# A two-headed kernel: the stage that prepares the tables is rewritten, and its rounds get other PSUM places and other side work

## The chip, the core and the metric

The kernel runs on one core of a Trainium2 chip. The metric is device time in microseconds (us), of one launch. PE is the matrix engine (TensorE), DVE the vector engine, ACT the scalar engine, POOL GpSimd, and SP the engine that mostly issues DMAs. SBUF is the on-chip memory, and PSUM is the small memory that matmuls write to: eight banks of 2 KB per partition, handed out here as "places" that must be emptied before they are written again.

## The reference, cut to what matters

Two independent heads, whose outputs are set side by side.

```
# A: 64 segments of 32 rows, one after the other; mem (8 rows) is carried over
h = concat([mem, x[segment]]); q, k, v = h@Wq, h@Wk, h@Wv
p = softmax(mask(q @ k.T * scale)); o = (p @ v) @ Wo
mem = o[:8]; out_a[segment] = o[8:]
# B: a long convolution of u with a kernel K that is made from D x N complex parameters
K[d, l] = Re sum_n C*exp(dt*A*l)*dt*B        # l = 0..2047, d = 0..1023, n = 0..127
y = irfft(rfft(K, 4096) * rfft(u, 4096))[:2048] + u * Dskip
```

Shapes: x and u are 2048 x 1024, the projection weights 1024 x 4096 each, A, B and C 1024 x 128 each, all in bf16.

## The kernel before, in words

The program runs head B first (`part_b`) and head A after it (`part_a`). While B runs, work for A that doesn't depend on the carried memory is done beside it (class `Ahead`): x is transposed, and of each segment the last 8 rows ("left rows", 24 to 31) are multiplied by Wk, Wv and Wq there; the 24 other rows are stored transposed in DRAM (`VXd`) and loaded by part A. Everything is emitted under a manual schedule: each engine runs its instructions in the order in which the code writes them, and so does each queue of DMAs.

The time of `part_b` falls into four stages.

**Parameter stage** (lines 703 to 918). The six parameter arrays are loaded (L710) as 128 partitions x 8 x 128 in pieces of 128 elements. From them DVE and ACT work out, in float32 on 128 x 1024 elements, five quantities: `x1` (decay), `x2` and `x6` (turn of one step, and of 16 steps), `x4` (logarithm of the modulus of C*B*dt) and `x3` (its angle). `put3` (L718) splits each into three bf16 parts, high, middle and low (L720, L723, L725, L729), and writes them to the DRAM tensors `PB`. Small arrays of table rows, `RE` and `RT`, are built by DVE (`rows`, L804, and L821 to L837). `matrices` (L761) makes the Fourier matrices `MF` (16 column groups, cosine and sine, 128 x 512 each): DVE multiplies (L776), ACT rounds (L778), DVE subtracts (L771) and takes absolute values (L767), ACT takes sines (L768, L772). `Ahead.transposes` (L95) loads x in 16 blocks of 128 rows on POOL's queue (L99), PE transposes each block in eight matmuls (L109), ACT copies the 24 other rows of each segment to `xst` (L112) and the left rows to `xTl` (L113), and SP's queue writes `xst` to `VXd` (L114). `Ahead.projections` (L117) is a generator of 96 projection groups: a group is 8 matmuls of 512 columns (keys and queries, L169) or 16 of 256 (values, L156) into one PSUM place, a weight slice of 512 KB (L127) serves two groups, and an eviction by ACT or DVE (L178, L163) follows. It begins once x is transposed, and runs ten groups in this stage (L910 to L918).

**Rounds** (L1275 to L1307). Sixteen rounds make K's values, 64 channels each, and carry side work. What a round does is written out by hand in the string `ORDER` (L658): each word is one step, in the order of emission, and a prime means that the step belongs to the round before.
- `X0p` to `X7p`: two matmuls of 324 columns into the place `pa` (L1204); `E0` to `E7`: ACT's exponential of it (L1212).
- `X0t` to `X7t`: one matmul of 456 columns into the place `ptt` (L1198); `n0` to `n7`: DVE takes the low 16 bits as a fraction of a turn (L1220).
- `S`, `C`: sine and cosine on ACT (L1225, L1234); `b`: absolute value (L1231), `w`: minus (L1238), `gi`, `gr`: products (L1186, L1187), on DVE; `K`: 128 small matmuls that sum over n (L1016), `x`: their copy out by DVE (L1024).
- `P0` to `P5`: six projection groups, `p0` to `p5` their evictions (ACT p0, p2, p3, p5; DVE p1, p4).
- `U0` to `U3`: four groups of the transform of u (8 matmuls, L975); `A0`, `A1`: ACT copies of the first two (L983); `u0`, `u1`: DVE sums and differences of the other two (L986, L987). After every fourth, POOL combines the four in six operations (`classes`, L956 to L959) and writes them to `Ud`. The last combination is put off to the end (`sums`, L1348).
- `M`: eight transposes of Fourier matrices (L944), copied out by `m` on DVE.

PSUM's eight banks: four places for P, U, K and M (`ps_k`), two for phases (`ptt`), and one of two banks for exponents (`pa`). Each round's parameters (`par_t`) are loaded from `PB` on POOL's queue (L1002), one round ahead; each of u's four column quarters is loaded whole, two buffers in turn (L933).

**Tail and pointwise stage.** After the sixteenth round the last products are made (L1320 to L1345), spectra of K are built, and 16 steps multiply them with u's transform (L1380 to L1386, weights L1159, spectrum matmuls L1175).

**Inverse transform**, and then **part A**, from about 660 us on; the diff touches neither.

Of the kernel before, what the change touches and what calls it, by code (L numbers as in the profile page):

```python
# [12 lines left out]
I32 = mybir.dt.int32  # L13
# [61 lines left out]
class Ahead:  # L75
# [19 lines left out]
    def transposes(self, pool, ps, ident):  # L95
        nc = self.nc
        def load(b):
            xb = pool.tile([128, self.Dm], BF16, name="xb", tag="xb")
            nc.gpsimd.dma_start(out=xb[:], in_=self.x[b * 128:(b + 1) * 128, :])  # L99
            return xb  # L100
        xbs = [load(b) for b in range(3)]
        yield
        for b in range(self.S // 128):
            if b + 3 < self.S // 128:
                xbs.append(load(b + 3))
            xb = xbs[b]
            pt = ps.tile([128, self.KC, 4, self.SL], BF16, name="pt_x", tag="ptx")
            for kc in range(self.KC):
                nc.tensor.transpose(out=pt[:, kc, :, :].rearrange("p a b -> p (a b)"), in_=xb[:, kc * 128:(kc + 1) * 128], identity=ident[:])  # L109
            yield  # L110
            xst = pool.tile([128, 4, self.KC, self.XM], BF16, name="xst", tag="xst")
            nc.scalar.copy(out=xst[:].rearrange("p s k r -> p k s r"), in_=pt[:, :, :, 0:self.XM])  # L112
            nc.scalar.copy(out=self.xTl[:, :, 4 * b:4 * b + 4, :], in_=pt[:, :, :, self.XM:self.SL])  # L113
            nc.sync.dma_start(out=self.VXd[4 * b:4 * b + 4, :, 256:].rearrange("s p f -> p s f"), in_=xst[:].rearrange("p s k r -> p s (k r)"))  # L114
            yield

    def projections(self):  # L117
# [3 lines left out]
        slices = [(m, t, c) for m, t, cs in (("k", 0, (0, 8)), ("v", 0, (0, 4)), ("q", 0, (0, 8)), ("v", 0, (4, 8)), ("k", 1, (0, 8)), ("v", 1, (0, 4)),  # L121
                                             ("q", 1, (0, 8)), ("v", 1, (4, 8))) for c in range(*cs)]
# [7 lines left out]
        take, vals = yield  # L130
        late = []
# [15 lines left out]
        for i, (m, t, c) in enumerate(slices):  # L147
# [3 lines left out]
            for j in range(2):  # L151
                a = take([128, 512], F32, "pro")
                if m == "v":
# [5 lines left out]
                    def evict(copy, a=a, t=t, c=c, j=j):  # L159
                        for _ in range(min(2, len(late))):  # L160
                            late.pop(0)()
# [5 lines left out]
                else:  # L167
# [4 lines left out]
                    def evict(copy, a=a, m=m, t=t, g=g, h=h2 + j, mo=mo):  # L172
                        for _ in range(min(2, len(late))):
                            late.pop(0)()
# [489 lines left out]
def part_b(ctx, tc, u, A_re, A_im, B_re, B_im, C_re, C_im, log_dt, Dskip, out_b, ahead, copies, residents, first_state):  # L664
# [28 lines left out]
    def take(shape, dtype, name):  # L693
        return ps_k.tile(shape, dtype, name=name, tag="s")
# [1000 lines left out]
```

## Time and profile before

| | us |
|---|---|
| median of three timed runs | 2002.03 (1999.43 to 2004.33) |
| the profiled execution's own time | 2001.01 |
| its span, first to last instruction | 1999.3 |
| PE busy | 1831.9 |
| DVE busy | 1413.8 |
| ACT busy | 960.1 |
| POOL busy | 416.9 |

The profile names an instruction by line, engine, operation and tiles. "Busy" is the time in which an engine had an instruction in it; successive instructions overlap by about 0.1 us, so that durations add up to somewhat more than the time they take in a row. A row of the view in order of time gives the start, the time to the end of the last of the merged instructions, and their count (x8); in brackets stands the idle time of the engine ahead of it and what ended it. A row of the view by stages gives, for one stretch, each engine's busy time with its count, the granted TensorE clock (1.00 is full speed), the share of time in which the 16 DMA engines were busy (modelled, so that it can pass 1), and GB/s.

### The profile page before, as it was taken

What the parts mean: (1) busy time and instruction counts of PE and PEld (TensorE: products, weight loads), DVE (VectorE), ACT (ScalarE), POOL (GpSimd) and SP (SyncE); (2) the same over time, 40 slices, a digit from 0 to 9 for tenths busy, and PEclk for the clock granted to TensorE, in tenths of its full rate; (3) what the DMA queues carried; (4) which work ended last, traced back from release to release, by engine and by line L of the source; (5) the groups of instructions that cost most, each with busy time, mean ns of one, the idle gap of its engine ahead of it and who ended that gap; (6) DMA issues with size and microseconds to landing.
All of it is one profiled execution on the core that took longest, in us unless ns stands there. A gap on an engine that the chain in (4) does not pass through costs nothing.

```text
span 1999.3 us, 74588 instructions
## 1 busy us (share of the span) xinstructions
PE 1831.9 (92%) x31956; PEld 1131.2 (57%) x31956; DVE 1413.8 (71%) x3441; ACT 960.1 (48%) x1673; POOL 416.9 (21%) x851
## 2 busy tenths in 40 slices
PE   1589999978999799999999999999999999999999
PEld 1365766645888455555555555555555555555554
DVE  8779999988995366666666666666766666666650
ACT  4888989872223243434343434444343444444330
POOL 2126454533100011111111111111111111111120
PEclk9699999977999899999999999999999999999999
DMA  6688997748768999999999999999999999999991
GB/s 173 179 229 266 266 267 204 193 117 278 216 203 260 328 327 340 341 331 349 340 340 335 351 337 342 346 342 349 348 348 342 337 347 340 349 342 349 344 339 42
DMA packets 348484, 588.69 MB, mean 294 GB/s; under 512 B 109880, under 2 KB 225928, under 8 KB 346104
## 3 DMA queue, kind: packets, MB, share of 16 engines
q1 hardware_dynamic: 294764, 526.35, 78.0%
q10 hardware_dynamic: 44812, 28.26, 4.6%
q0 software_dynamic: 8576, 29.32, 4.2%
q8 instruction: 250, 4.10, 0.8%
q14 instruction: 82, 0.67, 0.1%
HBM read 528.25 MB, written 66.05 MB: 297 GB/s over the span
## 4 chain that ended last, share of the span: by engine, by line
PE 39%; DMA 21%; DVE 3%; issue 1%; ACT 1%; POOL 0%; SPq 0%; DVEq 0%; POOLq 0%
PE acc L376 23%; DMA wst<-WD_v 8%; PE pp L489 8%; DMA wst<-WD_o 7%; PE pe L626 3%; PE tr L387 2%; DMA wst<-WD_k 2%; DMA arena<-PKd 2%; DMA wst<-WD_q 2%; PE pv L457 1%; DVE arena L583 1%; PE sc L401 1%; PE pv L461 1%; ACT arena L583 1%; PE tro L589 1%
## 5 line engine op out<-in xcount | busy, mean ns | idle before, releaser
L376 PEld LDWEIGHTS <-a_hT 128*32 128x32 bf16 x12352 | 328.0, 96 | 313.6 <-issue 57.0
L382 ACT CAST arena<-acc 128x512 bf16<-128x512 f32 x384 | 225.1, 586 | 393.9 <-PE acc L376 314.6
L489 PEld LDWEIGHTS <-arena 128*32 128x32 bf16 x8256 | 216.3, 96 | 86.9 <-issue 62.5
L376 PE MATMUL acc<-wst,a_hT 128*32 128x512 bf16 x2304 | 230.2, 382 | 23.9 <-DMA wst<-WD_v 20.5
L390 POOL COPY arena<-arena 128x128 bf16<-128x128 bf16 x128 | 37.3, 292 | 825.0 <-DMA arena<-PKd 277.9
L297 DVE TENSOR_SCALAR arena<-keep 128x256 int32<-128x256 int32 (+1 forms) x512 | 175.7, 395 | 27.6 <-PE acc L376 27.2
L376 PE MATMUL acc<-XM,a_hT 128*32 128x512 bf16 x2560 | 185.9, 381 | 0.0
L169 PE MATMUL pro<-XM,wsl 128*128 128x512 bf16 x512 | 119.5, 389 | 10.4 <-ACT XM L113 8.1
L489 PE MATMUL pp<-W_o,arena 128*32 128x256 bf16 x3584 | 122.8, 274 | 4.7 <-DMA W_o<-in_A_Wo_dram 4.6
L416 DVE TENSOR_REDUCE a_mx<-sc 128x4 f32<-128x160 f32 (+1 forms) x192 | 71.7, 374 | 74.9 <-PE sc L404 74.9
L420 ACT ACTIVATE sc<-sc 128x160 f32<-128x160 f32 (+1 forms) x192 | 63.9, 333 | 125.5 <-DVE sc L417 124.9
L376 PE MATMUL acc<-W,a_hT 128*32 128x512 bf16 x1536 | 119.4, 382 | 0.1
L504 DVE COPY arena<-tr 128x512 bf16<-128x512 bf16 x64 | 27.2, 425 | 126.8 <-PE tr L387 126.8
L424 DVE TENSOR_REDUCE a_mx<-sc 128x4 f32<-128x160 f32 (+1 forms) x192 | 72.8, 379 | 55.5 <-ACT sc L420 55.2
L1212 ACT ACTIVATE E<-pa 128x648 bf16<-128x648 f32 x128 | 91.1, 711 | 29.2 <-PE pa L1204 24.1
L1436 PE MATMUL yp<-Bt,MI 128*128 128x256 bf16 x680 | 104.5, 273 | 0.0
L376 PE MATMUL acc<-g,a_hT 128*32 128x512 bf16 x1024 | 102.6, 382 | 0.0
L451 POOL TENSOR_TENSOR arena<-arena,a_BD 128x128 bf16<-128x128 bf16 x128 | 51.1, 399 | 236.8 <-DVE arena L434 232.4
L583 ACT CAST arena<-pp 128x128 bf16<-128x128 f32 x64 | 17.0, 266 | 160.2 <-DVE arena L583 160.2
L489 PE MATMUL pp<-wst,arena 128*32 128x256 bf16 x1536 | 76.5, 275 | 17.3 <-DMA wst<-WD_o 14.4
L169 PEld LDWEIGHTS <-wsl 128*128 128x128 bf16 x512 | 51.1, 100 | 72.9 <-issue 18.5
L376 PE MATMUL acc<-wq,a_hT 128*32 128x512 bf16 x1024 | 91.4, 382 | 0.0
(338 smaller groups left out, 4100.2 us busy)
## 6 DMA issues: line engine op xcount, KB each, us to landing
wst<-WD_v SPq DMA_DIRECT2D x256, 512.0 KB
wst<-WD_k SPq DMA_DIRECT2D x192, 512.0 KB
wst<-WD_o SPq DMA_DIRECT2D x192, 512.0 KB
wst<-WD_q SPq DMA_DIRECT2D x128, 512.0 KB
Ud<-ux POOLq DMA_DIRECT2D x16, 1024.0 KB, 5.9
wq<-Ud SPq DMA_DIRECT2D x32, 512.0 KB
wsl<-in_A_Wk_dram SPq DMA_DIRECT2D x16, 512.0 KB
wsl<-in_A_Wv_dram SPq DMA_DIRECT2D x16, 512.0 KB
```

Of the source, the lines that this page charges most:

```text
L169: nc.tensor.matmul(a[:], lhsT=w[:, kc, 128 * j:128 * j + 128], rhs=xTl[:, kc, :, :].rearrange("p s k -> p (s k)"), start=(kc == 0), stop=( ...
L297: nc.vector.tensor_scalar(out=out.bitcast(I32), in0=in_.bitcast(I32), scalar1=0, scalar2=None, op0=ALU.bitwise_or)
L376: nc.tensor.matmul(a[32 * g:32 * g + 32, o_:o_ + rhs.shape[1]], lhsT=hT[:, kc, :], rhs=rhs, start=(kc == 0), stop=(kc == KC - 1), tile_pos ...
L382: nc.scalar.copy(out=q, in_=a[:])
L416: nc.vector.tensor_reduce(out=m_, in_=x, axis=AX.X, op=ALU.max)
L420: nc.scalar.activation(out=flat(sc, i), in_=flat(sc, i), func=ACT.Exp, scale=scale)
L424: nc.vector.tensor_reduce(out=m_, in_=x, axis=AX.X, op=ALU.add)
L489: nc.tensor.matmul(po[32 * qt:32 * qt + 32, o_:o_ + rhs.shape[1]], lhsT=oT[:, h % 4, (h % 16) // 4, :], rhs=rhs, start=False, stop=(h == 3 ...
L583: (nc.scalar.copy if j else nc.vector.tensor_copy)(out=osb[:, 128 * j:128 * j + 128], in_=pp[:, 1, 128 * j:128 * j + 128])
L626: nc.tensor.matmul(pe[n][:], lhsT=left[2 * b + hi // 16][:, 128 * (hi % 16):128 * (hi % 16) + 128], rhs=wo[u][:, 1024 * hh + 512 * n:1024 ...
L1212: sc.activation(out=T["E", r, e // 4][:, lo:lo + 8 * NE].rearrange("p (i c) -> p i c", i=2), in_=T.pop(("p", r, e))[:, :, 0:4 * NE], func= ...
L1436: pe.matmul(yp[:, b, :], lhsT=m_[:, b, cs, kc, :], rhs=Bt[:, kc, j, half, c_, :], start=(kc == 0 and cs == 0 and half == 0), stop=(kc == 3 ...
```

## The change

Parameter stage:
- x is no longer transposed whole. Four loads bring the left rows alone (128 rows each, on SP's and ACT's queues), PE turns them in 32 transposes (`T`), DVE copies them to `xTl` (`c`). The 24 other rows of each segment go to the rounds (`R`, `r`): one block of 96 rows a round, loaded on SP's queue, eight transposes of 96 columns, one DVE copy, one write to `VXd`.
- The parameter arrays and `PB` are laid out with 8 successive channels per partition, so that a partition's 8 x 128 elements are one piece of 2 KB in DRAM. The loads are spread over SP's and ACT's queues.
- The Fourier matrices come from 32 matmuls with 7 rows each (`F`, 512 columns) into PSUM places, whose low 16 bits ACT turns into sines (`f`); the DVE and ACT steps of `matrices` go.
- The arithmetic is cut: dt is taken into the logarithm (`lnd`), the reciprocal becomes exp(-ln), multiplications by constants join other operations, and three products or differences go to POOL (`Wi1`, `s1`, `lo1`).
- 21 projection groups run in this stage, not 10. The order of all of it is one string, `PAR`; a slash means the other engine (DVE for ACT, POOL for DVE or the reverse).

Rounds: `ORDER` is new. Five projection groups a round, all evicted by ACT (`p4` in the next round); U's copies are `u0`, `u2` on ACT, its sums `u1`, `u3` on DVE. Exponents get two places of two banks, phases one, the others three (in the parameter stage four). u comes in pieces of one class of rows and one column quarter, five buffers. The order of the weight slices is changed. Of the writes that wait in the list `late`, none goes out in the parameter stage, three per projection eviction in round 0 and two after that.

Tail: the last combination of u's classes is made by DVE and not by POOL, ahead of the second spectrum; the spectra use the two exponent places; later builds have three places, not four; `rows4` is another piece of memory.

The diff's core:

```diff
-ORDER = ("X0t' w0' X1t b0' C0' b1' P3' P1 P5' X0p' gi0' P0 C1' gr0' p3' n0 P2 E0 X1p X2t p5' E1 p1 U2' n1 p0 X2p E2 A1' w1' U3' gr1' X3p E3 "
-         "U0 n2 X4p gi1' X3t p2 E4 u1' X4t K0' X5p U1 n3 X5t n4 A0 E5 X6p X6t x0' M' n5 X7t n6 E6 X7p P4' K1' u0 n7 p4' E7 x1' S0 m' S1").split()
-ON_ACT = (('p0', 'P', 0), ('p2', 'P', 2), ('p3', 'P', 3), ('p5', 'P', 5), ('A0', 'U', 0), ('A1', 'U', 2))
-ON_DVE = (('p1', 'P', 1), ('p4', 'P', 4), ('u0', 'U', 1), ('u1', 'U', 3), ('m', 'M', 0))
+ORDER = ("U0 b0' U1 u0 w0' X0p' gi0' b1' u1 X0t' w1' p4 C0' C1' X1p gr0' P0 U2 n0 P1 gr1' X1t n1 u2 p0 E0 E1 gi1' P2 p1 X2t n2 X2p U3 X3p "
+         "K0' E2 X3t X4p p2 u3 E3 R n3 X5p X4t x0' n4 E4 r X6p E5 M X7p X5t E6 P3 E7 n5 X6t m S0 n6 K1' X7t x1' p3 n7 P4 S1").split()
+ON_ACT = (('p0', 'P', 0), ('p1', 'P', 1), ('p2', 'P', 2), ('p3', 'P', 3), ('p4', 'P', 4), ('u0', 'U', 0), ('u2', 'U', 2))
+ON_DVE = (('m', 'M', 0), ('r', 'R', 0), ('u1', 'U', 1), ('u3', 'U', 3))
+PAR = ("F0 rt F1 F2 F3 f0 T0 f1 T1 F4 c0/ f2 T3 f3 a2 Wi2/ F5 F6 F7 f4 f5 c3/ F8 f6 F9 c1/ T2 F10 Wi1 f7 f8 F11 f9 F12 c2/ t1 P0 f10 a1 "
+       "f11 f12 t2 e0 F13 P1 t3 F14 f13 P2 uv Wr1 Wi/ e1 f14 Wr2 F15 P3 Wr hi1 e2/ sq2 f15 F16 e3/ sq1 sm mx f16 P4 pr/ lns s1 t4 P5 mi1 "
+       "lo1 lnm P6 P7 ex e4/ e5/ e6/ hi2 p P8 ra t5 m q4 e7 F17 at s2 P9 e8 xr b1 f17 F18 e9 f18 mi2 P10 e10/ F19 P11 F20 lo2 f19 hi4 b2 "
+       "e11 P12 f20 F21 hi6 b3 f21 e12 F22 f22 q3 hi3 P13 s4 F23 s6/ e13 P14 f23 F24 mi4 s3 lo4 P15 F25 mi6 e14 mi3 f24 e15 P16 f25 e16 "
+       "F26 f26 F27 F28 f27 P17 F29 P18 f28 e17 f29 F30 f30 F31 f31 e18 P19 lo6/ P20 lo3 e19 rp e20").split()
...
-    PB = [dram.tile([PARTS[q], 8, 128, 128], BF16, name="PB%d" % q) for q in range(2)]
+    PB = [dram.tile([PARTS[q], D, 128], BF16, name="PB%d" % q) for q in range(2)]
...
-    ps_k = ctx1.enter_context(tc.tile_pool(name="b_psk", bufs=4, space=PSUM, side="right"))
+    ps_k = ctx1.enter_context(tc.tile_pool(name="b_psk", bufs=3, space=PSUM, side="right"))
...
-    ps_t = ctx_p.enter_context(tc.tile_pool(name="b_pst", bufs=2, space=PSUM))
-    ps_e = ctx_p.enter_context(tc.tile_pool(name="b_pse", bufs=1, space=PSUM))
+    ps_e = ctx_p.enter_context(tc.tile_pool(name="b_pse", bufs=2, space=PSUM))
+    ps_t = ctx_p.enter_context(tc.tile_pool(name="b_pst", bufs=1, space=PSUM))
...
+    def load_uv(dq, r):
+        if dq < 4:
+            uv[dq, r] = up.tile([128, 4, DQ], BF16, name="uv", tag="uv", bufs=5)
+            sy.dma_start(out=uv[dq, r][:], in_=u_r[r][:, :, DQ * dq:DQ * dq + DQ])
...
+        def matrix(i):
+            mt = take([128, 512], F32, "mf")
+            pe.matmul(mt[:], lhsT=turns_l[:, i // 2, :], rhs=turns_r[:, i % 2, :], start=True, stop=True)
+
+            def evict():
+                sc.activation(out=MF[:, :, i // 2, i % 2, :], in_=mt[:].bitcast(I16)[:, 0:1024:2].rearrange("p (k n) -> p k n", k=4), func=ACT.Sin,
+                              scale=float(TWO_PI / 65536))
+            return evict
...
+        for b in range(NB):
+            xb = xbs.pop(0)
+            pt = take([128, self.KC, 128], BF16, "pt_x")
+            for kc in range(self.KC):
+                nc.tensor.transpose(out=pt[:, kc, 0:n], in_=xb[0:n, 128 * kc:128 * kc + 128], identity=ident[0:n, 0:n])
+
+            def evict(copy, b=b, pt=pt):
+                xst = pool.tile([128, 4, self.KC, self.XM], BF16, name="xst", tag="xst", bufs=1)
+                copy(out=xst[:].rearrange("p s k r -> p k s r"), in_=pt[:, :, 0:n].rearrange("p k (s r) -> p k s r", r=self.XM))
+                nc.sync.dma_start(out=self.VXd[4 * b:4 * b + 4, :, 256:].rearrange("s p f -> p s f"), in_=xst[:].rearrange("p s k r -> p s (k r)"))
...
-    s0 = ps_e.tile([128, 2, 512], F32, name="pa", tag="pa")
-    s1 = [ps_t.tile([128, 512], F32, name="ptt", tag="ptt") for _ in range(2)]
+    now = [[ps_e.tile([128, 2, 512], F32, name="pa", tag="pa")[:].rearrange("p h (c d) -> p h c d", c=2)] for _ in range(2)]
...
+    sums.pop()()
+    spectrum(0, 1, [now[1][0][:, half] for half in range(2)])
```

455 lines of the change are left out of this document (226 added, 229 removed).

## The prediction

> **What bounds the kernel now.** I read the view by stages first, because the page's chain of waits, followed back from the end, accounts for 65% of the span only: it stops near 680 us, in part A, which the diff doesn't touch. After the stretch and its length come the busy times of PE, PE's weight loads, DVE, ACT and POOL, the granted clock, the DMA share and GB/s.
>
> ```profile
> 0.00:103.23 103.23, 41.16 (x228) 23.32 (x229) 85.03 (x123) 69.28 (x86) 21.32 (x68) 0.83 0.69 176
> ...
> 244.91:264.86 19.95, 19.95 (x241) 11.58 (x240) 18.64 (x30) 17.86 (x21) 10.17 (x12) 1.00 1.06 267
> ...
> 436.09:500.00 63.91, 55.03 (x322) 35.95 (x322) 56.67 (x47) 21.08 (x42) 28.18 (x58) 0.73 0.72 231
> ```
>
> The parameter stage lasts until the first exponential (103.23 us). PE works in 41.2 of it, DVE in 85.0, ACT in 69.3: DVE's list bounds it. The second row is one round: PE is busy in all of it, DVE in 18.64, ACT in 17.86 us. That it is one round is seen in ACT's rows in order of time, where a round's first exponential follows a load of ACT's table:
>
> ```profile
> 103.23 0.71 ACT L1212 ACTIVATE E<-pa 128x648 bf16<-128x648 f32 x1
> ...
> 244.91 0.71 ACT L1212 ACTIVATE E<-pa 128x648 bf16<-128x648 f32 x1
> 245.52 0.58 ACT L178 CAST kst<-pro 128x512 bf16<-128x512 f32 x1
> ...
> 264.86 0.71 ACT L1212 ACTIVATE E<-pa 128x648 bf16<-128x648 f32 x1
> ...
> 404.55 0.71 ACT L1212 ACTIVATE E<-pa 128x648 bf16<-128x648 f32 x1
> ```
>
> So a round takes 19.95 us, and PE bounds it. Fifteen rounds lie between 103.23 and 404.55, 20.09 each: the early ones were a little longer, and I don't count on that.
>
> **Part 1, the parameter stage.** Prices from before: groups of this stage (busy time, mean ns), ACT's sines and narrow copies in the tail, then PE, DVE's first and last of 30 operations on table rows, and two stretches.
>
> ```profile
> L723 DVE TENSOR_TENSOR x<-x,hi 128x1024 f32<-128x1024 f32 x5 | 6.0, 1221 | 1.1 <-ACT hi L720 1.1
> L767 DVE TENSOR_SCALAR tm<-tm 128x1024 int32<-128x1024 int32 x8 | 5.5, 690 | 4.4 <-ACT XM L772 4.4
> L178 DVE CAST kst<-pro 128x512 bf16<-128x512 f32 x6 | 4.0, 684 | 0.0
> ...
> L112 ACT COPY xst<-pt_x 128x768 bf16<-128x768 bf16 x16 | 13.0, 814 | 2.2 <-DMA VXd<-xst 2.2
> ...
> L725 ACT CAST mid<-x 128x1024 bf16<-128x1024 f32 x5 | 5.2, 1044 | 2.1 <-DVE x L723 2.0
> ...
> L178 ACT CAST kst<-pro 128x512 bf16<-128x512 f32 x5 | 2.8, 565 | 0.0
> ...
> L862 ACT ACT_TABLE_LOAD x1 | 1.3, 1283 | 0.0
> ...
> L875 ACT ACTIVATE x<-x,magic 128x1024 f32<-128x1024 f32 x1 | 1.1, 1131 | 0.0
> ...
> L862 ACT ACTIVATE x<-x 128x1024 f32<-128x1024 f32 x1 | 1.1, 1057 | 0.0
> ...
> 429.37 2.69 ACT L1128 ACTIVATE g<-gf 128x512 bf16<-128x512 int16 x5
> ...
> 402.25 0.98 ACT L1124 COPY g<-gt 7x1024 bf16<-7x1024 bf16 x1
> ...
> 242.11 3.62 PE L169 MATMUL pro<-XM,wsl 128*128 128x512 bf16 x16
> ...
> 75.06 16.61 PE L169 MATMUL pro<-XM,wsl 128*128 128x512 bf16 x64 [8.11 <-ACT XM L113]
> ...
> 10.86 2.00 PE L109 MATMUL pt_x<-b_ident,xb 128*128 128x128 bf16 x16 [10.86 <-DMA xb<-in_A_x_dram]
> ...
> 8.43 0.15 DVE L809 TENSOR_SCALAR row<-pF 128x1 f32<-128x1 f32 x1
> ...
> 13.93 0.34 DVE L837 TENSOR_SCALAR RT<-RT,ang 128x456 bf16<-128x456 bf16 x1
> ...
> 40.00:60.00 20.00, 5.31 (x45) 4.55 (x43) 18.67 (x14) 11.51 (x19) 3.64 (x5) 0.66 0.69 184
> 60.00:80.00 20.00, 9.28 (x54) 5.17 (x52) 13.49 (x16) 15.02 (x25) 3.97 (x7) 0.59 0.97 242
> ```
>
> *ACT after:* 32 sines at 2.69/5 = 0.54 (17.2), ten part copies at 1.04 (10.4), two roundings at 1.13 (2.3), six functions at 1.06 (6.3), 15 evictions at 0.565 (8.5), three copies of turns at 0.98 (2.9), and, from the order of functions (exp, ln, sine, ln, exp, arctan, sine), seven table loads at 1.28 (9.0): 56.6 us.
> *DVE after:* I count 27 operations with two inputs of 128 x 1024 at 1.22 (33.0), two with one input at 0.69 (1.4), one in bf16 that I put at 0.7, four copies of left rows at 0.68 (the price of `ms`, below: 2.7), six evictions at 0.684 (4.1), the table rows, from 8.43 to 14.27 now (5.8), and some twenty operations on a few columns at 0.15 (3): 50.7. The reciprocal and all of `matrices` are gone.
> *PE after:* 21 groups. Two groups at full clock end in 3.62 us, less a tail of 0.16: 1.73 each. The eight from 75.06 on took 2.08 each, the clock being at 0.59 until 80. So 36.3 to 43.7; 32 matmuls of 512 columns at 1.73/8 (7.0), 56 transposes at 2.00/16 (7.0): 50 to 58.
>
> The three lists are nearly level. The longest, ACT's, begins with five DMA issues (at the 0.49 of SP's below, 2.5 us): it ends at 59 if nothing waits. PE can't begin a group before the last left rows are copied, by my count of DVE's order at 14 us; 14 + 36.3 + 18 of the sines' matmuls (4) is 54 at the least. Left rows and parameters (2.5 MB) are in by 10 us at the round's 267 GB/s.
>
> Then the hand-over. SP sends the last low part (`lo3`) only behind the weight load of group 20, which waits for group 19's matmuls: about 58 us. The rounds wait for this write and for the parameter load on POOL's queue. In before, with a DMA's size and its median us to landing in the last row:
>
> ```profile
> 74.24 0.49 SPq L730 DMA_DIRECT2D PB<-lo  x1
> ...
> 78.25 3.90 POOL L1002 DMA_DIRECT2D pt<-PB  x6 [7.31 <-DMA VXd<-xst]
> ...
> pt<-PB POOLq DMA_DIRECT2D x32, 72.0 KB, 5.0
> ```
>
> From the write's issue it is 4.0 us to the load's, then two issues of 0.65 and the landing of 5.0: 10.3. PE then owes a group and a U (half a group's columns: 2.6), ACT two evictions (1.2). 58 + 10.3 + 3.8 = 72. I add 2 for waits among three level engines, net of durations that overlap: **74, so -29**, between -17 (before, DVE's list filled only 85.0 of 103.2; a fifth of 57 lost is 11, and 3 of colder PE) and -36 (nothing lost, overlaps counted).
>
> What POOL's new operations do to DVE is seen in the tail, in rows in order of time:
>
> ```profile
> 436.09 1.22 DVE L1380 TENSOR_TENSOR z<-wq,pa 128x1024 f32<-128x1024 f32 x1 [2.45 <-PE pa L1175]
> ...
> 447.88 6.30 DVE L1159 TENSOR_TENSOR XM<-XM 128x1536 bf16<-128x1536 bf16 x1
> ...
> 460.57 0.95 DVE L1159 TENSOR_TENSOR XM<-XM,wq 128x1536 bf16<-128x1536 bf16 x1
> ...
> 448.08 1.28 POOL L956 TENSOR_TENSOR ux<-us 128x512 f32<-128x512 f32 x1
> ...
> 450.59 2.77 POOL L959 TENSOR_TENSOR ux<-us 128x256 f32<-128x256 f32 x4
> ...
> 454.24 4.02 PE L1175 MATMUL hps<-XM 128*128 128x256 bf16 x18 [1.85 <-DVE XM L1159]
> ```
>
> The same operation takes 0.95 us alone and 6.30 while POOL's six run. POOL's three new operations of 128 x 1024 (twice 1.28, so 2.6 each) may thus hold DVE by up to 7.7 us: DVE's 50.7 becomes 58.4, level with ACT, so it enters the range and not the sum. The Trainium skill has this as a rule: its page "GPSIMD Engine Reference" (section "Key points") says that POOL shares its SBUF interfaces with DVE and contends with DVE instructions that read two SBUF inputs. The trace agrees, with 6.30 against 0.95. For the hand-over, the rows at 40 and 60 us show clocks of 0.66 and 0.59 where PE worked in 5.3 and 9.3 of 20 us. The Trainium skill's page "TensorE: Matmul & The Clock Gate" (section "Part 1: The HAM clock gate") halves the clock after about 3.4 us of idleness. By it the wait for the parameter load would slow the next groups, an estimate of +2 us from that page, left out of the sum.
>
> **Part 2, the rounds.** PE loses the sixth group and gains eight transposes of 96 columns; DVE loses two evictions and gains `r`; ACT gains an eviction. Groups of the round from 244.91 on, and a phase matmul that waited:
>
> ```profile
> L1212 ACT ACTIVATE E<-pa 128x648 bf16<-128x648 f32 x9 | 6.4, 711 | 1.7 <-PE pa L1204 1.3
> L1220 DVE TENSOR_SCALAR nr<-ptt 128x456 f32<-128x456 int16 x9 | 5.5, 628 | 0.5 <-PE ptt L1198 0.4
> ...
> L944 PE MATMUL mt<-b_ident,XM 128*128 128x128 bf16 x8 | 0.6, 219 | 0.0
> ...
> L948 DVE COPY ms<-mt 128x1024 bf16<-128x1024 bf16 x1 | 0.7, 682 | 0.0
> ...
> 395.02 0.35 PE L1198 MATMUL ptt<-RT,pt 128*128 128x456 bf16 x1 [0.44 <-DVE nr L1220]
> ```
>
> PE: 19.95 - 1.73 + 0.36 (0.6 less the tail, by 96/128) = 18.6. ACT: 17.86 + 0.58 = 18.4. `r` lies between 0.51 (`ms`, 0.68 for 1024, by 768 elements) and the 0.81 that ACT took for this copy (L112), so DVE: 18.64 - 2 x 0.69 + 0.51 to 0.81 = 17.8 to 18.1. ACT's 1.3 us of waits for `pa` go with the second place; PE stays the longest. But in place of PE alone three engines bound the round within 0.8 us, with one phase place (each `n` must end before the next phase matmul) and 13 takings of three places. Walking through ORDER with these durations, each `n` has another DVE operation ahead of it, and only `n6`, behind group P3, waits visibly (0.6). I take **18.9, so 15 x 1.05 = -16**, between -22 (18.6, and the early rounds' surplus) and -3 (19.75).
> DMA: x rows and `VXd` writes come in (6 MB), 2.75 MB of weights leave: at the 184 GB/s of the row at 40 us, when such writes ran, 33 - 15 = 18 us at most over 15 rounds. The round above had a DMA share of 1.06 and no idle PE: weight slices, loaded three ahead, are its cover. Without it the 18 us are on the path.
>
> **Part 3, the tail.** POOL's `sums` held the weighting for 5.3 us, yet PE stood idle for 1.85 only. On DVE the six cost some 2.5 (half of 1.22 twice, a quarter four times), in its gap of 2.45 before 436.09. I take **-2**, between -6 and +4 (three places for builds, a colder PE). In round 15 four narrow copies go from two engines to ACT, which sheds five evictions: nothing.
>
> **Sum:** 2001.0 (the profiled execution's own time, 1.0 below the median) - 29 - 16 - 2 = **1954**. Part A follows rigidly: its loads wait for memory that B frees.
>
> **Rivals.** *A, the rounds stay at 19.95.* A wait at some of the places handed over gives back the 1.05. For it: three level engines; against it: PE kept 19.95 of 19.95 beside 18.6 and 17.9. 1954 + 16 = 1970. If DMA holds the rounds, so that the change doesn't do in them what it is built for, it is this time too.
> *B, the parameter stage loses a fifth* (11 and not 2), with POOL in DVE's way (5 more): 1954 + 14 = 1968. Both: 1984.
> *C, slower: the single phase place.* If every `n` stands idle for the wait above (0.44) and the matmul (0.35), DVE's round is 17.95 + 8 x 0.79 = 24.3: 16 x 5.4 = +86, 2040. It decides from five exposed places in eight on (+2.9 a round, the whole 47). Against it: work stands between, and with two places such waits come to 0.4 a round.
>
> **How the numbers follow.** The forecast within its own bounds (1940 to 1963) 0.57, A 0.15, B 0.13, both 0.05, C 0.06, better than 1937 0.04. The range is 1937 (-36, -22, -6) to 1984 (A and B). A difference of 0.2% (4 us) is about what a measurement of this kernel can tell from no change. Faster 0.93, same 0.01, slower 0.06.
>
> **What would show it.** First exponential at 70 to 78 us, ACT busy in over 80% of that stage; first exponentials of successive rounds 18.6 to 19.2 apart, ACT at 95% or more; no idle time of 0.4 or more before most `n`; no DVE operation of 6 us in the tail; part A as long as now. I'm wrong if PE waits for weights in the rounds, if sines and groups starve each other of places, or if the first exponential comes after 85.

## The result, and the profile after

The changed kernel takes 1976.93 us (median of 4 runs, 1966.72 to 1981.25), the kernel before 2000.73 beside it: a ratio of 0.9872, 95% interval 0.9826 to 0.9918. A second set of 6 runs gave 1978.25 and 0.9875 (0.9843 to 0.9907). So the change saves 24 us where 47 were forecast: the time lies inside the stated range (1937 to 1984), but outside the forecast's own bounds (1940 to 1963). The profiled execution, the longest of the four, took 1981.25 us, with a span of 1979.5 (1999.3 before).

The view by stages of the changed kernel: the stage up to the first exponential, one round, and the stretch of the tail that lies as far behind the sixteenth exponential as the one shown of before. Columns are the stretch and its length, then the busy time and count of PE, PE's weight loads, DVE, ACT and POOL, granted clock, DMA share, GB/s.

```profile
0.00:87.68 87.68, 69.91 (x364) 36.51 (x365) 49.69 (x92) 56.86 (x82) 15.58 (x39) 0.86 0.67 195
281.68:300.43 18.75, 18.44 (x263) 13.20 (x262) 17.82 (x29) 18.07 (x22) 9.22 (x12) 1.00 0.89 229
408.29:472.20 63.91, 53.02 (x301) 33.95 (x300) 48.73 (x44) 18.90 (x38) 25.23 (x56) 0.73 0.73 232
```

The first stage lasts 87.68 us in place of 103.23, and now no engine fills it: PE works in 69.9, ACT in 56.9 (65%), DVE in 49.7. A round takes 18.75 us in place of 19.95, with PE, ACT and DVE busy in 18.4, 18.1 and 17.8 of it: three level engines. ACT's rows in order of time (start, time) give the rounds:

```profile
87.68 1.31 ACT L1242 ACTIVATE E<-pa 128x648 bf16<-128x648 f32 x2
...
163.45 1.31 ACT L1242 ACTIVATE E<-pa 128x648 bf16<-128x648 f32 x2
...
185.36 1.31 ACT L1242 ACTIVATE E<-pa 128x648 bf16<-128x648 f32 x2
...
204.62 1.31 ACT L1242 ACTIVATE E<-pa 128x648 bf16<-128x648 f32 x2
...
217.00 0.59 ACT L202 CAST kst<-pro 128x512 bf16<-128x512 f32 x1 [2.04 <-DMA PKd<-kst]
...
225.87 1.31 ACT L1242 ACTIVATE E<-pa 128x648 bf16<-128x648 f32 x2
...
376.72 1.31 ACT L1242 ACTIVATE E<-pa 128x648 bf16<-128x648 f32 x2
```

From the first exponential to the sixteenth there are 289.04 us (301.32 before). Rounds 5 and 7 are long: 185.36 - 163.45 = 21.91 and 225.87 - 204.62 = 21.25, where the steady ones take 18.32 to 18.76 (the eighth to the fourteenth), the first four 18.6 to 19.3 and the last 20.12.

Where the 19.8 us of the span come from, by the starts of the same instructions in the two traces: first exponential -15.6, fifteen rounds -12.3, so -27.8 at the sixteenth; first matmul of the inverse (`yp`) at 469.2 in place of 496.8, -27.6; first new state copied into `a_hT` at 672.9 in place of 699.3, -26.4; last one at 1897.8 in place of 1917.1, -19.3. The tail gave nothing, and 7 us went in part A, which the diff doesn't touch.

**The hand-over.** The forecast had lo3, the last part of the parameters, written at about 58, and its loads back in time for X0p' at 68. In order of time, all engines (SPq is SP's queue of DMA issues; in brackets the idle time ahead and what ended it):

```profile
52.98 5.85 SPq L879 DMA_DIRECT2D PB<-part  x4
...
57.45 1.04 ACT L884 CAST part<-x 128x1024 bf16<-128x1024 f32 x1 [3.06 <-DMA PB<-part]
...
58.52 1.23 DVE L894 TENSOR_TENSOR part<-x,part 128x1024 bf16<-128x1024 f32 x1 [2.93 <-ACT part L884]
...
63.96 0.37 SPq L150 DMA_DIRECT2D wsl<-in_A_Wv_dram  x1
...
64.58 3.83 SPq L188 DMA_DIRECT2D PVd<-vst  x2
...
69.01 0.41 SPq L150 DMA_DIRECT2D wsl<-in_A_Wv_dram  x1
69.51 0.64 SPq L879 DMA_DIRECT2D PB<-part  x1
...
75.11 3.23 POOL L1032 DMA_DIRECT2D pt<-PB  x6 [14.82 <-DMA PVd<-vst]
...
79.45 0.70 PE L1234 MATMUL pa<-RE,pt 128*128 128x324 bf16 x2 [7.47 <-DMA pt<-PB]
...
80.87 3.51 PE L180 MATMUL pro<-wsl,XM 128*128 128x256 bf16 x16
...
85.09 1.91 PE L180 MATMUL pro<-wsl,XM 128*128 128x256 bf16 x16
```

DVE had lo3 at 59.75, 1.7 us behind the 58 at which the forecast had its write issued, because ACT had waited 3.06 us for a place of the middle parts whose last write was not out. SP sent it at 69.51 only: three V writes, each waiting for a group of PE and its eviction, two weight loads, the first of which (63.96) waited 3.4 us for PE, and lo6 stood ahead of it. From there to X0p' it is 9.94 us (10.3 forecast), but PE had idled 7.47 us, its next group took 3.51 in place of 1.91, and 8.23 us pass to the first exponential where 3.8 were reckoned.

**The rounds.** SP's queue and PE in round 5 of the changed kernel, in order of time, and three stretches of the view by stages (140 to 220 holds the fourth to the seventh round, 260 to 320 steady ones):

```profile
139.50 1.31 SPq L150 DMA_DIRECT2D wsl<-in_A_Wq_dram  x1
...
154.30 2.28 SPq L150 DMA_DIRECT2D wsl<-in_A_Wq_dram  x1
...
159.39 3.53 SPq L135 DMA_DIRECT2D VXd<-xst  x1
...
164.09 1.90 PE L193 MATMUL pro<-XM,wsl 128*128 128x512 bf16 x8 [3.27 <-DMA wsl<-in_A_Wq_dram]
```

```profile
140.00:180.00 40.00, 36.30 (x479) 21.98 (x477) 35.51 (x65) 35.66 (x43) 19.67 (x29) 1.00 0.99 276
180.00:220.00 40.00, 37.31 (x529) 26.95 (x528) 36.62 (x61) 35.99 (x42) 18.30 (x24) 1.00 0.99 290
260.00:320.00 60.00, 59.06 (x788) 40.08 (x786) 57.13 (x91) 57.98 (x69) 28.70 (x38) 1.00 0.85 236
```

PE waited 3.27 us for a slice of W_q though slices are loaded three ahead. It is the sixth of W_q's eight. There are four places, so that its own was free when the second one's groups ended, at 136.9, but its load left at 154.30: behind the fifth one's load (139.50) SP's queue sent two copies of weights, four copies of `PVd` into `VXd` and two pieces of u first, one after the other. The write of 512 rows that took SP 3.53 us (159.39) stands behind this load, and so can't have held it. In round 7 it is ACT (the row at 217.00 above): 2.04 us for the staging buffer `kst`, whose last rows were still on their way to PKd. The DMA engines are busy for 0.99 of the time from 140 to 220 and 0.85 from 260 to 320.

**Part A.** The copies of the new state, first and last start, of before, of the changed kernel, and of its second profile:

```profile
L591 DVE COPY a_hT<-tro x126: 174/175/175, 699.3 to 1917.1; 128x32 bf16<-128x32 bf16 x126
```
```profile
L615 DVE COPY a_hT<-tro x126: 173/175/175, 672.9 to 1897.8; 128x32 bf16<-128x32 bf16 x126
```
```profile
L615 DVE COPY a_hT<-tro x126: 165/175/176, 670.4 to 1886.0; 128x32 bf16<-128x32 bf16 x126
```

62 segments take 1217.8, 1224.9 and 1215.6 us.

### The profile page after: what moved, and what is told of

Its sections match the earlier page's. It is cut to its first block, busy times and chain, and to the rows that moved or that the text cites. A ratio compares the mean times of both kernels' runs of the same rounds, so it can differ in the third digit from the quotient of the medians.

```text
span 1979.5 us, 74742 instructions
## 1 busy us (share of the span) xinstructions
PE 1840.5 (93%) x32044; PEld 1132.6 (57%) x32044; DVE 1364.1 (69%) x3402; ACT 950.4 (48%) x1681; POOL 397.6 (20%) x837
## 4 chain that ended last, share of the span: by engine, by line
PE 36%; DMA 26%; DVE 2%; ACT 1%; issue 1%; ACTq 0%; POOL 0%; SPq 0%; DVEq 0%; POOLq 0%
PE acc L400 21%; DMA wst<-WD_v 10%; DMA wst<-WD_o 9%; PE pp L513 7%; PE pe L650 3%; PE tr L411 2%; DMA wst<-WD_q 2%; DMA wst<-WD_k 2%; DMA out_dram<-arena 2%; DMA arena<-PKd 1%; DVE arena L607 1%; PE pv L481 1%; ACT arena L607 1%; PE pv L485 1%; PE sc L425 1%
## 5 line engine op out<-in xcount | busy, mean ns | idle before, releaser
L400 PE MATMUL acc<-wst,a_hT 128*32 128x512 bf16 x2304 | 228.9, 381 | 27.2 <-DMA wst<-WD_v 19.3
L1250 DVE TENSOR_SCALAR nr<-ptt 128x456 f32<-128x456 int16 x128 | 80.3, 628 | 31.2 <-PE ptt L1228 28.3
```

What stands on the lines that cost most here:

```text
L400: nc.tensor.matmul(a[32 * g:32 * g + 32, o_:o_ + rhs.shape[1]], lhsT=hT[:, kc, :], rhs=rhs, start=(kc == 0), stop=(kc == KC - 1), tile_pos ...
L1250: v.tensor_scalar(out=T["n", r, e // 4][:, lo:lo + 8 * NT], in0=T.pop(("t", r, e))[:, 0:8 * NT].bitcast(I16)[:, 0:16 * NT:2], scalar1=floa ...
```

## The experiments

The theory after this comparison: the miss has three sources of their own, the hand-over through SP's queue, transfers in rounds 5 and 7 that fill the DMA engines, and the length of part A, which wanders. Rivals: PE's own list would have ended as late; the long rounds are a matter of SP's order and not of bytes; the change lengthens part A. The starts of all runs (us; "sum" is the fifteen rounds, "part A" the first to the last copy of the state; the ratio is to the kernel before, run beside each set: its median was 2000.73 to 2007.11, so that across sets ratios compare and medians don't; sets are the first two rows, e0 to e3, e4 to e7, e8 to e10 and e11):

| kernel | first exp. | sum | sixteenth | part A | median, n | ratio (95%) |
|---|---|---|---|---|---|---|
| before | 103.23 | 301.3 | 404.55 | 1217.8 | 2000.73, 4 | 1 |
| changed | 87.68 | 289.0 | 376.72 | 1224.9 | 1976.93, 4 | 0.9872 (0.9826 to 0.9918) |
| e0 changed again | 86.10 | 289.4 | 375.52 | 1215.6 | 1978.25, 6 | 0.9875 (0.9843 to 0.9907) |
| e1 last parts on POOL | 78.14 | 297.0 | 375.18 | 1224.5 | 1970.24, 6 | 0.9838 (0.9805 to 0.9871) |
| e2 = e1, third part place | 81.09 | 289.7 | 370.77 | 1213.2 | 1966.55, 6 | 0.9819 (0.9786 to 0.9852) |
| e3 x rows on POOL | 83.84 | 409.1 | 492.95 | 1226.8 | 2087.02, 4 | 1.0396 (1.0346 to 1.0445) |
| e4 copies from round 7 | 88.64 | 291.8 | 380.46 | 1225.1 | 1977.88, 4 | 0.9848 (0.9818 to 0.9878) |
| e5 old slice order | 88.21 | 285.6 | 373.85 | 1225.9 | 1976.72, 6 | 0.9849 (0.9815 to 0.9883) |
| e6 = e1 and e4 | 77.16 | 291.7 | 368.87 | 1219.4 | 1964.99, 5 | 0.9779 (0.9752 to 0.9807) |
| e7 sums on POOL | 88.39 | 289.0 | 377.43 | 1220.4 | 1974.81, 1 | |
| e8 = e1 and e5 | 78.05 | 286.7 | 364.75 | 1226.1 | 1969.07, 6 | 0.9814 (0.9784 to 0.9844) |
| e9 = e8, third part place | 77.12 | 289.2 | 366.33 | 1216.6 | 1972.57, 6 | 0.9836 (0.9802 to 0.9869) |
| e10 = e9, copies spread | 81.73 | 286.3 | 368.05 | 1221.9 | 1966.43, 5 | 0.9802 (0.9773 to 0.9832) |
| e11 = e8, copies spread | 76.18 | 288.8 | 364.99 | 1223.2 | 1965.19, 6 | 0.9796 (0.9763 to 0.9829) |

**e0: the changed kernel once more.** No edit.

> The changed kernel, not altered. The diff doesn't touch part A's 62 segments between the first and the last copy of a new state into a_hT; they took 1217.8 us in the profiled execution before and 1224.9 after. Theory (part A's length wanders from execution to execution with the transfers, the 7 us are chance): this profile shows another length, anywhere from 1215 to 1228, with the first exponential again at 87.7 +-0.5 and the sixteenth at 376 to 378. Rival (the change makes part A longer by 7 us, through memory or through the place of its tables): 1224 to 1226 again. Ratio to the kernel before 0.985 to 0.990 by either.

First exponential 86.10, sixteenth 375.52, part A 1215.6. So part A's 7 us more are not the change's doing at that size: two executions of one kernel differ by 9.3, and the eleven altered kernels span 1213.2 to 1226.8. Their mean with the two, e3 left out, is 1221.4. With one profile of before, at 1217.8, a lengthening by some 4 us can't be told from chance and stays open. A gain of a few us is to be read at the sixteenth exponential and not from one total.

**e1: the last two parts go out on POOL's queue.**

```
-            sy.dma_start(out=PB[q][row + i]...
+            (gp if i == 2 and k in "63" else sy).dma_start(out=PB[q][row + i]...
```

> The writes of lo6 and lo3 to PB go out on POOL's queue, which stands idle there, instead of SP's, where they were issued at 68.50 and 69.51, lo3 10 us after DVE had made it. Theory (the hand-over was late because the two writes stood behind weight loads and PVd writes on SP): lo3's write goes out at 59.8 to 60.5, the rows of pt land near 70, PE goes from its last u group (ends 71.98) to X0p' without the idle 7.5 us and at a higher clock, first exponential at 75 to 79, whole kernel 9 to 12 us below the changed one. Rival (SP was only one of several: PE's list, the weights behind its groups, or the loads of pt end as late anyway): first exponential at 83 or later, under 5 us gained.

In order of time, the hand-over of e1:

```profile
60.96 0.56 POOL L879 DMA_DIRECT2D PB<-part  x1 [3.77 <-DMA PB<-part]
...
65.03 3.34 POOL L1032 DMA_DIRECT2D pt<-PB  x6 [2.24 <-DMA PB<-part]
...
70.44 1.91 PE L1003 MATMUL ups<-uv,XM 128*128 128x256 bf16 x16
...
72.19 0.44 PE L1234 MATMUL pa<-RE,pt 128*128 128x324 bf16 x2
...
76.84 1.28 ACT L1242 ACT_TABLE_LOAD   x1
...
78.14 1.31 ACT L1242 ACTIVATE E<-pa 128x648 bf16<-128x648 f32 x2
```

lo3 leaves at 60.96, X0p' follows PE's list without a gap, the first exponential comes at 78.14: the theory's case, and SP's queue priced at 8.0 to 9.5 us. The later runs bear it out: the first exponential comes at 76.18 to 81.73 in all seven kernels with this edit, and at 86.10 to 88.64 in the five executions with the two writes and x's rows on SP's queue. From X0p' 5.95 us pass, of which 1.28 are the load of ACT's table. But the sixteenth exponential comes at 375.18, where the changed kernel's two executions have it at 376.72 and 375.52: rounds 5 and 7 took 24.88 and 25.87. In this execution a head start of 8 us was all but gone at the eighth exponential. PE and the stretches around its wait in round 5:

```profile
154.76 2.31 PE L193 MATMUL pro<-XM,wsl 128*128 128x512 bf16 x5 [3.44 <-DMA wsl<-in_A_Wq_dram]
...
158.53 2.85 PE L193 MATMUL pro<-XM,wsl 128*128 128x512 bf16 x8
```
```profile
152.00:156.00 4.00, 1.24 (x3) 0.43 (x4) 2.72 (x5) 3.24 (x5) 0.57 (x2) 0.70 1.17 271
156.00:160.00 4.00, 3.78 (x10) 1.51 (x10) 1.22 (x2) 0.58 (x1) 0.00 (x0) 0.50 1.12 335
```

The wait is for a slice of W_q again (3.44 us), with the DMA engines at 1.17 and 1.12, and the clock falls to 0.50 behind it, so that the next group takes 2.85 us. But this execution (1977.42) is the longest of e1's six, and e0's profiled one (1970.26) the shortest of its six. By medians e1 is 8.0 us ahead (1970.24 against 1978.25), as much as the head start, though the intervals of the ratios overlap. So the trace shows that the rounds can take the head start back, and not that they do so as a rule.

**e2: a third buffer for the middle parts, on top of e1.**

```
-                parts[k, i] = parh.tile(sh, BF16, name="part", tag="part%d" % i, bufs=(3, 2)[i])
+                parts[k, i] = parh.tile(sh, BF16, name="part", tag="part%d" % i, bufs=(3, 3)[i])
```

> As the last parts on POOL's queue, and a third buffer for the middle parts, for which ACT waited 3.06 us at 54.4 and PE behind it 2.55 us. Theory (that wait is on the path to the first exponential): another 2 to 3 us earlier than with POOL's queue alone, first exponential at 72.5 to 77. Rival (the wait is covered, PE's groups 19 and 20 wait for weights then): within 0.7 us of it.

```profile
58.84 1.23 DVE L894 TENSOR_TENSOR part<-x,part 128x1024 bf16<-128x1024 f32 x1 [3.35 <-DMA PB<-part]
...
60.38 0.56 POOL L879 DMA_DIRECT2D PB<-part  x1 [3.79 <-DVE row L826]
...
65.29 1.91 PE L1003 MATMUL ups<-uv,XM 128*128 128x256 bf16 x16
...
66.61 3.37 POOL L1032 DMA_DIRECT2D pt<-PB  x6 [4.38 <-DMA PB<-part]
...
73.28 0.70 PE L1234 MATMUL pa<-RE,pt 128*128 128x324 bf16 x2 [6.08 <-DMA pt<-PB]
```

PE's list ended 5.1 us earlier (67.2), but X0p' waited 6.08 us for the loads of `pt`, since lo3's write left hardly earlier (60.38 for 60.96) and took 5.7 us to the loads in place of 3.5. ACT's wait of 3.06 us was gone, but in its place DVE waited 3.35 us ahead of lo3 until a write to `PB` had landed; the low parts have two places. A miss for both sides: the wait was real, and what it hid was the next wait and the way through memory. The sixteenth exponential came at 370.77, 4.4 us ahead of e1's, though the first one came 3 us behind it. Beside the changed kernel's two executions e2 is 5.0 and 6.6 us ahead at the first exponential and 4.8 and 6.0 at the sixteenth: with the same order of slices it kept its head start.

**e3: x's rows on POOL's queue.**

```
-                nc.sync.dma_start(out=xb[0:n], in_=x_s[4 * b:4 * b + 4, 0:self.XM, :])
+                nc.gpsimd.dma_start(out=xb[0:n], in_=x_s[4 * b:4 * b + 4, 0:self.XM, :])
...
-                nc.sync.dma_start(out=self.VXd[4 * b:4 * b + 4, :, 256:]..., in_=xst[:]...)
+                for o in (0, 2):
+                    nc.gpsimd.dma_start(out=self.VXd[4 * b + o:4 * b + o + 2, :, 256:]..., in_=xst[:, o:o + 2]...)
```

> The changed kernel, with the loads of x's other rows and the writes of their transposes (in two halves) on POOL's queue instead of SP's. Theory (the two rounds of 21.9 and 21.3 us are long because SP stood 3.5 us in one such write and the weight slices behind it came late): no round but the last over 20 us, fifteen rounds in 284 to 286.5 instead of 289.0, whole kernel 2.5 to 4 us below the changed one. Rival (the DMA engines themselves are full there, or the long rounds fall elsewhere from execution to execution): two or three rounds over 20.5 us again, fifteen in 288 to 291.

Neither: after the first, rounds of 25 to 32 us, 110 us slower than the changed kernel. POOL's rows of one round, and the view of waits from 200 to 400:

```profile
323.34 0.74 POOL L136 DMA_DIRECT2D VXd<-xst  x1
329.57 0.73 POOL L136 DMA_DIRECT2D VXd<-xst  x1 [5.49 <-issue]
332.06 0.72 POOL L121 DMA_DIRECT2D xb<-in_A_x_dram  x1 [1.76 <-PE pa L1235]
337.00 0.58 POOL L981 DMA_DIRECT2D MId<-ms  x1 [4.22 <-issue]
```
```profile
PE ptt L1229 <- DVE nr L1251: 54.6, 15, 7.7
DVE ms L980 <- DMA MId<-ms: 54.3, 8, 7.8
...
POOL VXd L136 <- issue: 42.4, 7, 8.1
POOL MId L981 <- issue: 40.2, 7, 7.4
```

Between one half of 256 short rows and the next, and ahead of the next DMA, POOL stands still for 4.2 to 8.1 us with nothing that the profile shows to wait for. The write of `ms` behind it comes late, DVE's copy into `ms` waits for its buffer, and PE waits for DVE's `nr`. What e3 was to tell (SP's order or bytes) it leaves open; its theory, the write of 3.5 us ahead of the slice, the rows of round 5 above rule out for that round of the changed kernel.

**e4 and e5: which bytes fill rounds 5 and 7.** In e4 the eighteen copies of weights wait until round 7; in e5 the slices of V come in fours again.

```
-        if copies:
+        if copies and r >= 7:
```
```
-        ... ("k", 0, (0, 8)), ("v", 0, (0, 8)), ("q", 0, (0, 8)), ("v", 1, (0, 3)), ("k", 1, (0, 8)), ("v", 1, (3, 6)), ...
+        ... ("k", 0, (0, 8)), ("v", 0, (0, 4)), ("q", 0, (0, 8)), ("v", 0, (4, 8)), ("k", 1, (0, 8)), ("v", 1, (0, 4)), ...
```

> The changed kernel, with the eighteen copies of weights in memory (WD) and into the low blocks, two a round at the sines, issued from round 7 on instead of from round 0. With POOL's queue for the last parts the first exponential came 8 to 9.5 us earlier (78.14) and the eighth no earlier than 223.96 (225.87 and 224.65 in two executions of the changed kernel): rounds 5 and 7 took 24.9 and 25.9. Theory (the transfers of the first seven rounds bound them: copies, V rows and weight slices together keep the DMA engines at 0.99 to 1.04 from 140 to 240): with the copies gone from there, rounds 5 and 7 take 18.7 to 20, the sixteenth exponential comes 3.5 to 6 us earlier than 375.5 to 376.7, at 370 to 373, unless the later rounds pay. Rival (the long rounds are a matter of SP's queue, one write of 3.5 us ahead of a weight slice, and not of bytes): both stay over 20.5.

> The changed kernel with the order of the weight slices of before (V's slices in fours between K and Q), so that the first rows of V come together two groups of sixteen slots later and their eight 256 KB copies into VXd leave the stretch 132 to 154. Theory (bytes in the first seven rounds, to which these copies and the PVd writes ahead of them belong): rounds 5 and 7 shorten to under 20, the long ones come later or not at all, sixteenth exponential 2 to 5 us earlier. Rival (the order of slices is not what fills the DMA engines; the copies of WD do it alone): rounds 5 and 7 within 1 us of 21.9 and 21.3, or others as long in their place.

In e4 rounds 5 and 7 take 19.22 and 19.00 (the sixth slice of W_q leaves at 148.00, and its group waits for nothing), but rounds 11, 12 and 15 take 22.19, 20.65 and 21.83: moved and not saved, the sixteenth exponential 3.7 us later. In e5 rounds 5 and 7 take 19.25 and 19.02 with the copies where they were, nothing but the last goes over 19.5, and fifteen take 285.6 (-3.4). The stretches that the changed kernel's rows above show, in e4:

```profile
140.00:180.00 40.00, 39.03 (x491) 23.30 (x489) 38.14 (x68) 38.24 (x44) 20.82 (x30) 1.00 0.81 241
180.00:220.00 40.00, 39.22 (x543) 28.36 (x541) 38.07 (x64) 38.29 (x44) 18.84 (x24) 1.00 0.90 253
260.00:320.00 60.00, 56.34 (x762) 38.88 (x761) 52.07 (x83) 52.80 (x63) 28.75 (x38) 0.94 0.93 262
```

With the copies gone the share falls from 0.99 to 0.81 and 0.90, and rises later from 0.85 to 0.93. So either load taken away frees rounds 5 and 7, here and in all five later runs with one of the two edits (19.23 to 19.26 and 19.00 to 19.03). Whether by its bytes or by its entries on SP's queue, these two runs don't tell, since both go together: in e5 the DMA share stayed at 1.02 and 1.00 there, and no round was long. Full DMA engines alone aren't enough, then. That it counts which transfers stand ahead of the slice that is due fits the late load above (154.30); more than that stays open.

**e6: e1 and e4 together.**

> The last parts on POOL's queue and the copies from round 7 on, both. Theory (the two add up once the DMA engines have room in the first rounds): first exponential at 77 to 79, fifteen rounds in 283 to 287, sixteenth exponential at 361 to 366, 10 to 14 us below the changed kernel, 1963 to 1967 by the runs here. Rival (the first rounds stay bound by transfers without the copies too): sixteenth at 369 or later and under 7 us gained.

First exponential 77.16; rounds 5 and 7 19.23 and 19.00, rounds 11, 12 and 15 22.53, 19.43 and 22.08; sixteenth 368.87. In between: the head start now lasts (11.5 us beside e4 at the first exponential, 11.6 at the sixteenth), and the late copies cost some 6 us in rounds 11, 12 and 15 beside the changed kernel's 18.75, 18.70 and 20.12.

**e7: the last sums on POOL, as before.**

```
-                            sums.append(lambda: classes(v, kc, dq, got[2], s_))
+                            sums.append(lambda: classes(gp, kc, dq, got[2], s_))
```

> The changed kernel with the last six sums of the classes on POOL, as before, instead of DVE. Forecast: the move was to save the 6.30 us that one DVE operation took beside them in place of 0.95, 2 us net of DVE's own six. Theory (DVE's six additions cost as much as they save, the tail is bound elsewhere): from the sixteenth exponential (376.72) to the first matmul of the inverse (469.2), 92.5 us in the changed kernel and 92.3 before, within 0.7 us of 92.4 here, with one DVE operation of about 6 us back. Rival (they save 2 us and something else in the tail lost them): 94 to 95.

From the sixteenth exponential to the first inverse matmul 470.2 - 377.4 = 92.8 us (92.5 in the changed kernel): the move is worth nothing that one execution can show. But no DVE operation of 6 us came back. POOL ran the six from 388.60 on, ahead of DVE's weighting and not beside it:

```profile
388.60 1.28 POOL L987 TENSOR_TENSOR ux<-us 128x512 f32<-128x512 f32 x1
```
```profile
416.14 0.96 DVE L1189 TENSOR_TENSOR XM<-XM 128x1536 bf16<-128x1536 bf16 x1 [0.54 <-ACT XM L1180]
```

In before the inputs of these sums were ready at 419.0, but POOL ran them at 448.08, behind twenty writes of `Kd` that the code gives it first; in the changed code, and in e7, the sums are emitted ahead of those writes (and u's last group comes earlier too). The new place in the order, and not the engine, took away the 6.30.

**e8 to e11: the pieces together.** e8 is e1 and e5, e9 adds e2's buffer, e10 adds to e9 the copies at `if copies and (h == 0 or r >= 12)`, e11 is e10 without the buffer.

> The last parts on POOL's queue and the old order of weight slices, both. With the new order the 8 to 10 us by which POOL's queue brought the first exponential forward were lost again in rounds 5 and 7; with the old order no round but the last took over 19.5. Theory (it was the bytes of V's early copies that took the head start): first exponential at 77 to 79, fifteen rounds in 285.5 to 288, sixteenth exponential at 363 to 367, whole kernel 10 to 13 us below the changed one, about 0.982 of the kernel before. Rival (with the head start the transfers bind the first rounds in any order): fifteen rounds at 291 or more, sixteenth at 369 or later.

> As the one before it, and a third buffer for the middle parts. The third buffer took away ACT's wait of 3.06 us and brought PE's list from 72.3 to 67.2, but the first exponential came later with it (81.09 beside 78.14), lo3's write taking 5.9 us to land instead of 3.8. Theory (the way of lo3 through memory ends last now, and PE waits cold for it): first exponential at 77 to 81 again, no better than without the buffer by more than 1 us. Rival (the late landing was chance): 73 to 76, and 2 to 4 us gained.

> As the one before it, and the eighteen copies of weights spread: one a round at the first sine, two from round 12 on, instead of two a round in the first nine. Theory (the rounds wait only where the DMA engines are full; with the copies spread they never are): every round but the last between 18.6 and 19.3, fifteen in 283 to 285.5, another 1 to 3 us. Rival (what is left over 18.7 in the first seven rounds is V's evictions and queue order, not bytes; or the copies now meet the keys' stores at the end and lengthen rounds 12 to 15): within 1 us of the one before it or slower.

> The last parts on POOL's queue, the old order of weight slices and the copies spread, with two buffers for the middle parts again: each piece that shortened a stage in the runs so far, and not the third buffer, with which lo3's way through memory took longer in two of three executions. Theory (the pieces act in different stages and add): first exponential at 77 to 79, fifteen rounds in 285.5 to 287, sixteenth exponential at 363 to 366, ratio to the kernel before 0.977 to 0.982. Rival (the spread copies or the hand-over pay elsewhere): sixteenth at 368 or later, ratio 0.983 or more.

e8 keeps the head start: first exponential 78.05, sixteenth 364.75, 12.0 us ahead of the changed kernel's. Its long round is the first (20.91; 20.60 in e9, 21.89 in e11, where ACT stood 3.31 us ahead of a copy into `kst` at 89.21). The old order brings W_q's first eviction to the staging buffer eight groups sooner, when K's rows may not be out yet; that this is what ACT waited for is argued from the code and not shown. Nor is the old order free of waits for slices: in e9 PE waited 2.99 us for a slice of W_k, and the eighth round took 21.66. The third buffer brings 0.9 us in e9 and in e10 a late first exponential again (X0p' waited 5.27 us), so it stays undecided. Spreading the copies left the rounds at 286.3 and 288.8 (286.7 in e8), with 19.98 and 19.83 in the eleventh: no gain there. So e8 and e11 came as their theories had them, and e10's rounds missed theirs. By ratio e6, e10 and e11 (0.9779 to 0.9802) are the best versions here, some 0.7 to 1% under the changed kernel's 0.9875; their intervals overlap each other's and those of e2 and e8, so that these five can't be told apart.

## Why the forecast was half right

That the time fell inside the range is partly luck. The range reached 1984 by rivals A and B together; A (rounds at 19.95) and POOL in DVE's way (in B) did not come about, and what filled their room was a late hand-over, two long rounds and, in the profiled execution, part A. Two of the forecast's own signs of being wrong came: PE waited for weights in a round, and the first exponential came after 85.

- **First exponential, 74 (bounds 67 to 86) forecast, 87.68 and 86.10 measured.** This is the step that failed: the write of lo3, sent at "about 58 us", and then 10.3 and 3.8. The write went out at 69.51. The forecast had put it behind one weight load; SP's queue held it behind two loads, lo6 and three V writes that waited for PE and ACT. e1 prices that at 8.0 to 9.5 us, colder groups included. Not all of the miss is SP's queue: X0p' was forecast at 58 + 10.3 = 68.3 and came at 79.45, and in e1, right behind PE's list, at 72.19. So of the 13.7 us some 7.3 are the queue, 3.9 a longer list of PE and 4.4 the way from X0p' to the exponential, less the 2 that had been added for waits.
- **3.8 from X0p' to the exponential were 8.23:** the load of ACT's table (1.28) and the three matmuls ahead of the group (0.75 in e1) had been left out, and PE was cold: behind the idle 7.47 us the granted clock was 0.53 from 79.45 to 84.40. e1, without the idle time and at a clock of 1.00, needs 5.95, so the cold clock costs 2.3. The estimate of +2 us from the Trainium skill's page "TensorE: Matmul & The Clock Gate" (section "Part 1: The HAM clock gate"), which had been left out of the sum, agrees with these 2.3.
- **ACT at 56.6 us was to bound the stage** and was busy in over 80% of it by forecast; it was busy in 65%, though its list came out at the length forecast (56.9). PE's was the longest: its first group of products began at 19.34, behind the last of the left rows (14 in the forecast), and from there to 72.0 PE was busy in 49.3 of 52.7 us. Only then did it wait for memory, the 7.47 us.
- **POOL's three operations** took 2.12 to 2.39 us (2.6 taken) and held DVE by almost nothing (one operation of 1.36 in place of 1.21); the 7.7 of the range didn't come. While they ran, DVE mostly waited for PE or copied out of PSUM, so that the case of the tail, 6.30 against 0.95, was hardly put to the test.
- **The hand-over by itself**, 10.3 forecast, took 9.94. Right.
- **Rounds at 18.9: right as a mechanism and in size,** 18.75 in the steady ones, PE 18.44, ACT 18.07, DVE 17.82 of it. Rival A (19.95) and rival C (the single phase place, +5.4) did not come about; the one wait that shows before an `n` is that of n6, forecast at 0.6 and seen at 0.69 to 0.71. Fifteen gave -12.3 in place of -16. The cover named for the transfers, "weight slices, loaded three ahead", failed in round 5 (PE's 3.27 us), and in round 7 ACT waited for a buffer on its way out; the two rounds took 3.2 and 2.5 us more than a steady one. e4 and e5 name transfers without which they don't.
- **Tail -2: measured +0.2.** The long DVE operation went (0.96 in place of 6.30) and the stretch is as long as ever; it had been covered.
- **Part A rigid:** right within what one execution can show; the 7 us lost in the profiled one are part of its spread (e0).

The sum for the profiled execution: 13.7 at the first exponential, 3.7 in the rounds, 2.2 in the tail and 7.1 in part A make 26.7 of the 27.3 us between 1954 and 1981.25. The first is the step at fault; the fourth lies within the spread of one kernel's executions, and the median is 4.3 us under this execution.

The forecast also added the parts as if a gain in the first stage were kept, and that isn't certain. The eighth exponential came at 225.87, 224.68 and 223.96 where the first had come at 87.68, 86.10 and 78.14 (the changed kernel twice, e1): in e1's profiled execution the transfers of the first seven rounds took the head start back, and the sixteenth exponential moved by under 2 us. In e2, with the same order of slices, it was kept, and e1's median has it too. With the copies late (e6 beside e4) the sixteenth moved by 11.6 us, and in the old order (e8 beside e5) by 9.1. How often the new order takes a head start back, one profile of each kernel doesn't tell.

## What to carry to other kernels

Ask of a short write that ends a chain which queue issues it and what the entries ahead of it wait for; a wait of a neighbour on the same queue is on the path. A gain ahead of a stretch that waits for transfers may be taken back there, in one execution and not in another: read a change at several fixed points along the kernel, and compare two runs of one kernel before explaining a few us of its last stage.

## What the hardware showed beside that

- With the write of x's rows on POOL's queue, in halves of 256 rows, POOL stood still for 4.2 to 8.1 us behind a DMA (e3, from 200 to 400 us), and what followed on it came late; SP issued all 512 rows of the same write in 0.36 to 3.53 us (the least and the most of 16 in the changed kernel).
- The clock falls after short waits, but not after each: of the four waits for a W_q slice in round 5, of 3.02 (e0), 3.26 (e2), 3.27 (changed) and 3.44 us (e1), the clock of the lowest stretch of 4 us fell to 0.50 to 0.69 behind three and stayed at 1.00 behind that of 3.27. The Trainium skill's page "TensorE: Matmul & The Clock Gate" (section "Part 1: The HAM clock gate") gives a free-running window of some 3.4 us; a window that runs free would explain why the length of the wait alone doesn't decide, but no run here shows it.
